# Four loads tied to the products of earlier chunks, two loads cut in half, and a relu ahead of a conversion

## The chip, the core and the metric

The kernel runs on one core of a Trainium2 chip. The metric is the device time of one execution in microseconds. The core has five engines with an instruction stream each: TensorE (PE in the profile; its weight loads are listed apart as PEld), VectorE (DVE), ScalarE (ACT), GpSimd (POOL) and SyncE (SP). SP does no arithmetic here, it issues every DMA of the kernel, one after the other in the order of its stream. The transfers themselves run on 16 DMA engines.

## The reference

A retention layer (a linear recurrence over 768 steps, 4 batches, 8 heads of dimension 64) is followed by a feed-forward layer with a relu, a convolution over three time steps and a sigmoid gate.

```python
def _attn_ref(q, k, v):
    gamma = 1.0 - 2.0 ** (-5.0 - np.arange(H))
    state = np.zeros((B, H, D, D))
    for t in range(S):
        state = gamma[None, :, None, None] * state + np.einsum('bhd,bhe->bhde', k[:, :, t], v[:, :, t])
        y[:, :, t] = np.einsum('bhd,bhde->bhe', q[:, :, t], state) / np.sqrt(D)
    return y

def _moe_ref(x, w_in, conv_w, w_out):
    h = np.maximum(x @ w_in, 0.0)            # [4, 768, 512] @ [512, 1024]
    conv_out = sum over k of conv_w[k] * (h shifted by k - 1 along time, zero at the ends)
    gate = 1.0 / (1.0 + np.exp(-conv_out))
    return h * gate @ w_out                  # [1024, 512]
```

The weights arrive as float64 and are converted on the chip.

## The kernel before, in words

The retention is computed in chunks of 64 time steps. A chunk number n stands for two batches and 64 steps, so there are 24 chunks. For a chunk, four blocks lie side by side in one tile `rw`: q and k with the head dimension on the partitions (slots 0 and 1), and k and v with time on the partitions (slots 2 and 3); a fifth slot takes the state carried over from the chunk before. One slot pair, 0 and 1 or 2 and 3, is 512 KB. There are three `rw` tiles, used in turn, so a chunk takes the tile of the chunk three before it.

The steps of chunk n, by their names in the code:

- `load/n` (L342) brings slots 0 and 1 for the first four chunks and for the chunks in `IN_TWO`, and all four slots (1 MB) for the others. `load_kv/n` (L352) brings slots 2 and 3 where `load` brought half.
- `scores/n` (PE, L410, tile `ps_s`) multiplies k by q. For the chunks from 4 on these products are emitted inside `mix/(n-1)`. There is one `ps_s` buffer: `scores/n` can start only when `masked/(n-1)` has read it.
- `masked/n` (DVE, L437) puts the masked scores back into slot 1; `scale_v/n` (ACT, L378) scales v in slot 3.
- `mix/n` and `across/n` (PE, L410, tiles `ps_y` and `ps_st`) make the output of the chunk and add to the state; `carry/n` (ACT, L444) copies the state; `decay/n` (DVE, L451), `x_head/n` (ACT, L461) and `x_rest/n` (DVE, L467) turn the output into two parts, a rounded one and the rest, for the next layer.

The weights are loaded in 16 pieces (`load_w/0` to `/7` the first matrix, `/8` to `/15` the second; `/16` is the convolution). Piece i goes through a row of conversions: `w_abs/i` (ACT, L495), `w_clamp/i`, `w_shift/i`, `w_sign/i`, `w_power/i` (DVE, L500 to L521), `w_head/i` (ACT, L546), `w_low/i`, `w_rest/i`, `w_add/i` (DVE, L529, L561, L576).

The first product `mm1/u/f` (PE, L590, tile `ps_m`) works on units u of two chunks and on pieces f of the weights; `relu/u/p` (ACT, L602) empties a `ps_m` buffer, of which there are two. Convolution, gate and second product follow and are not touched by the change.

At the very start PE has nothing to multiply, so six products on zeros are emitted (`fill`, L330), and three more ahead of `mix/0` (L324).

The order of all steps is written out by hand as the string `ORDER`: the steps are emitted in that order, and each engine executes its own instructions in the order in which they were emitted. An instruction waits only for the data and the buffers it needs. Besides this there is a table `HELD`: a step that stands in it as a key waits in addition until the last instruction of the step named beside it has finished. All keys of it are DMA loads. As SP works through its stream in order, whatever is queued on SP behind a held load waits too.

Of the kernel before, what the change touches and what calls it, by code (L numbers as in the profile page):

```python
# [61 lines left out]
HELD = {  # L62
    "load_kv/2": "mix/0", "load_kv/3": "make_gy/0", "load/7": "w_low/4", "load_w/4": "w_abs/3",
# [22 lines left out]
    w_shift/0 w_sign/0 w_abs/1 w_power/0 w_head/0 w_clamp/1 w_rest/0 scores/0 w_low/0 masked/0 scale_v/0 w_add/0
    w_shift/1 w_abs/2 mix/0 w_sign/1 w_clamp/2 w_shift/2 carry/0 load_kv/2 scores/1 w_power/1 load/3 w_head/1
    load_w/3 masked/1 load_w/16 scale_v/1 w_low/1 w_sign/2 mix/1 decay/0 across/1 make_gy/0 carry/1 w_head/2
    w_rest/1 load_kv/3 scores/2 load/4 decay/1 scale_v/2 masked/2 x_head/0 w_add/1 scores/3 x_head/1 w_power/2
    w_abs/3 x_rest/0 mix/2 x_rest/1 load_w/4 w_clamp/3 across/2 scale_v/3 w_shift/3 masked/3 mm1/0/0 load/5 w_low/2  # L90
    load_w/5 w_rest/2 mm1/0/1 w_sign/3 decay/2 w_head/3 w_add/2 carry/2 mix/3 w_abs/16 w_power/3 w_abs/4 w_rest/3
    across/3 x_head/2 masked/4 relu/0/0 w_low/3 mm1/0/2 load/6 scale_v/4 w_add/3 x_rest/2 mm1/0/3 carry/3 decay/3
    w_clamp/4 x_head/3 w_shift/4 mix/4 w_abs/5 x_rest/3 relu/0/1 w_clamp/5 across/4 make_gy/1 load_w/6 load_w/7
    mm1/1/0 w_shift/5 w_sign/4 w_sign/5 w_head/4 mm1/1/1 w_power/4 carry/4 w_power/5 w_head/5 masked/5 mm1/1/2
    scale_v/5 w_rest/4 w_clamp/16 w_low/4 relu/1/0 mm1/1/3 w_shift/16 load/7 scale_v/6 w_sign/16 w_add/4 w_power/16
    w_low/5 mix/5 relu/1/1 decay/4 w_abs/6 w_rest/5 across/5 w_clamp/6 w_low/16 w_add/5 mm1/1/4 carry/5 load/8
    decay/5 load_w/8 x_head/4 masked/6 w_abs/7 mm1/0/4 w_shift/6 w_add/16 w_sign/6 w_power/6 w_head/6 mix/6
    make_gy/2 conv_tap/0/2 across/6 w_clamp/7 scale_v/7 w_shift/7 masked/7 mm1/0/5 load/9 load_w/9 w_sign/7 carry/6
    conv_tap/0/3 w_low/6 mm1/1/5 relu/0/2 w_rest/6 w_head/7 seam/0/2/0 w_power/7 seam/0/1/0 w_add/6 mix/7 w_rest/7
    w_abs/8 across/7 w_low/7 x_head/5 relu/1/2 w_add/7 mm1/0/6 load/10 x_rest/4 w_clamp/8 x_rest/5 mm1/0/7 w_shift/8  # L100
    scale_v/9 w_sign/8 mm1/2/0 relu/0/3 masked/8 w_abs/9 scale_v/8 carry/7 mm1/2/1 w_power/8 w_head/8 load_w/10
    w_clamp/9 conv_tap/0/0 load_w/11 decay/7 mm1/1/6 w_shift/9 w_low/8 w_sign/9 mix/8 decay/6 w_head/9 scale_v/10
    across/8 masked/9 seam/0/0/0 seam/0/2/2 seam/1/2/0 mix/9 x_head/6 x_head/7 carry/8 w_power/9 relu/2/0
# [21 lines left out]
    conv_tap/1/6 gate/1/2 w_add/12 decay/14 diff/0/0/3 gated/1/2 seam/3/1/2 g_head/0/3 g_rest/0/3 conv_tap/1/2
    mm2/0/1/2/0 w_rest/15 w_add/15 conv_side/1/2/2 g_head/1/2 conv_tap/1/7 conv_side/1/6/0 masked/15 conv_tap/1/3
    scale_v/15 sum_w/0/7 conv_side/1/7/0 conv_side/1/6/2 relu/5/1 mm2/0/0/2/0 mm2/0/1/3/0 mm2/0/0/3/0
    conv_side/1/3/0 conv_side/1/7/2 conv_side/1/2/0 conv_side/1/3/2 gate/1/1 put/0/1/0 g_rest/1/2 gated/1/1
    g_head/1/1 load/16 mix/15 seam/6/3/0 seam/3/0/0 gate/1/3 across/15 carry/15 conv_tap/2/4 conv_tap/2/5 mm1/5/4
    mm1/5/5 seam/2/3/2 scale_v/16 diff/0/0/1 seam/3/2/0 mm2/1/0/0/0 g_rest/1/1 mm2/1/0/1/0 mm2/1/0/2/0 gated/1/3  # L130
    conv_side/2/4/2 sum_w/0/0 conv_tap/2/0 conv_side/2/0/2 g_head/1/3 g_rest/1/3 conv_tap/2/2 put/0/0/0 mm2/1/1/0/0
    mm2/1/1/1/0 diff/0/0/2 conv_side/2/5/2 sum_w/0/8 sum_w/0/9 conv_side/2/5/0 decay/15 conv_side/2/4/0 masked/16
    gate/2/2 conv_tap/2/1 head/0/0/0 decay/13 diff/0/1/3 conv_side/2/0/0 gated/2/2 g_head/2/2 diff/0/1/1
    conv_side/2/1/2 conv_side/2/1/0 conv_side/2/2/0 load/17 scale_v/17 g_rest/2/2 conv_tap/2/6 conv_tap/2/7
    conv_tap/2/3 mix/16 across/16 carry/16 relu/4/3 seam/3/3/2 head/0/1/0 gate/2/0 load/18 scale_v/18 mm2/1/1/2/0
    mm2/1/1/3/0 masked/17 mix/17 seam/5/3/2 seam/3/2/2 seam/5/2/2 seam/5/1/0 conv_side/2/7/0 conv_side/2/2/2
    across/17 conv_side/2/6/0 decay/16 conv_side/2/3/2 conv_side/2/3/0 gate/2/1 store/0/0/0 x_head/12 carry/17
    load/19 load_kv/19 masked/18 mm2/1/0/3/0 mix/18 across/18 seam/5/2/0 gated/2/1 g_head/2/1 seam/3/0/2 store/0/1/0
    gated/2/0 g_head/2/0 sum_w/0/1 put/1/1/0 store/1/1/0 g_rest/2/1 decay/17 relu/5/2 conv_tap/3/2 seam/6/1/0
    seam/4/3/0 seam/4/1/2 diff/0/1/2 g_rest/2/0 scale_v/19 put/1/0/0 store/1/0/0 conv_side/3/2/0 decay/18 diff/1/0/3  # L140
    x_head/13 conv_tap/3/4 conv_side/3/4/0 conv_tap/3/5 conv_side/3/5/0 carry/18 conv_tap/3/3 conv_side/3/3/0
    conv_side/2/7/2 conv_side/3/2/2 masked/19 load/20 conv_side/2/6/2 sum_w/0/2 conv_side/3/3/2 scale_v/20 gate/3/1
    gated/3/1 x_rest/13 mm1/5/6 load/21 mm1/5/0 mm1/5/1 mm1/5/7 head_rest/0/0/0 g_head/3/1 relu/5/0 mm2/2/0/0/0
    mm2/2/1/0/0 mm2/2/1/1/0 mix/19 masked/20 gate/2/3 conv_side/3/5/2 g_rest/3/1 across/19 mix/20 scale_v/21
    conv_tap/3/0 conv_tap/3/1 conv_side/3/4/2 decay/19 conv_side/3/0/2 gated/2/3 gate/3/2 conv_side/3/1/2
    conv_side/3/1/0 mm2/2/0/1/0 mm2/2/1/2/0 mm2/2/0/2/0 g_head/2/3 carry/19 sum_w/1/0 g_rest/2/3 mm2/2/0/3/0
    mm2/2/1/3/0 across/20 head/0/1/1 gated/3/2 conv_side/3/0/0 seam/5/1/2 relu/5/3 masked/21 conv_tap/4/0 g_head/3/2
    g_rest/3/2 gate/3/0 gated/3/0 x_rest/12 load/22 scale_v/22 conv_tap/4/1 mix/21 diff/0/1/4 conv_tap/4/2
    conv_side/4/2/2 g_head/3/0 g_rest/3/0 carry/20 across/21 conv_tap/3/6 seam/5/3/0 conv_tap/3/7 conv_side/4/1/0
# [5 lines left out]
    seam/5/0/0 gate/4/1 w_rest_t/0/1 sum_w/0/3 conv_tap/4/6 store/2/1/0 mm2/3/1/2/0 mm2/3/1/3/0 put/3/1/0 head/0/1/2
    conv_tap/4/5 conv_side/4/4/2 sum_w/0/4 conv_side/4/6/0 mix/22 masked/23 across/22 carry/22 store/3/1/0
    head/0/0/2 scale_v/23 w_head_t/1/1 conv_side/4/5/0 gated/4/1 decay/22 g_head/4/1 conv_side/4/4/0 mm2/3/0/3/0
    mm2/4/0/0/0 mix/23 seed/0/0 put/3/0/0 w_head_t/0/2 head/0/0/1 w_rest_t/1/1 sum_w/1/3 diff/1/1/3 sum_w/1/4
    w_head_t/1/2 across/23 decay/23 conv_side/4/5/2 conv_tap/4/7 prod/0/0/2 w_rest_t/1/2 g_rest/4/1 w_rest_t/0/2
# [727 lines left out]
```

## Time and profile before

| | |
|---|---|
| time of three executions | 329.06, 329.79 (median), 330.97 us |
| the profiled execution: own time, span | 330.33 us, 328.6 us |
| granted TensorE clock over the span | 0.999 of full speed |
| busy DVE, ACT, POOL | 288.3, 214.6, 25.8 us (88%, 65%, 8%) |
| DMA | 40.77 MB |
| idle time of PE before `ps_s` products, and whom it ended with | 1.7 us DVE, 1.0 us "issue" |
| idle time of DVE before `masked` | 5.1 us, ended by PE |

The span is what the profile covers; the execution's own time is 1.73 us longer. The busy time of an engine is the time in which one of its instructions runs. "Idle before" is the time for which an engine stood still ahead of an instruction, and the arrow names what ended it; "issue" means that the profile shows nothing that the engine waited for. Windows are given in microseconds from the start of the span.

### The profile page before, as it was taken

The numbers are of one execution on the slowest core, as the hardware profiler recorded it, in microseconds if no ns is written. First come the engines' busy times: TensorE is split into PE (matmuls) and PEld (weight loads), VectorE is DVE, ScalarE is ACT, GpSimd is POOL, SyncE is SP. The second block draws the span as 40 slices with busy tenths as digits, with TensorE's granted clock in tenths as the row PEclk, the third lists the DMA queues.
The fourth block names the chain that finished last, engine by engine and source line by source line (L and its number), as shares of the span: only waits on it lengthen the run. The fifth ranks groups of instructions, "written<-read, shape, count | busy, mean of one in ns | idle before, by whom it ended". The sixth has DMA issues, their size and how long they took to land.

```text
span 328.6 us, 10761 instructions
## 1 busy us (share of the span) xinstructions
PE 320.6 (98%) x4642; PEld 286.2 (87%) x4642; DVE 288.3 (88%) x566; ACT 214.6 (65%) x448; POOL 25.8 (8%) x100
## 2 busy tenths in 40 slices
...
GB/s 250 349 362 324 212 312 284 254 78 256 192 106 279 133 19 144 128 253 151 90 194 34 34 0 35 34 2 0 32 34 0 65 0 65 3 64 0 66 64 64
DMA packets 10559, 40.77 MB, mean 124 GB/s; under 512 B 1296, under 2 KB 1808, under 8 KB 8080
## 3 DMA queue, kind: packets, MB, share of 16 engines
...
q8 instruction: 36, 0.59, 0.7%
...
## 4 chain that ended last, share of the span: by engine, by line
PE 89%; DVE 8%; ACT 1%; issue 1%; ACTq 0%; DVEq 0%
PE ps_o L808 39%; PE ps_m L590 16%; PE ps_m L711 8%; PE ps_y L711 8%; PE ps_s L410 5%; PE ps_st L410 4%; PE ps_y L410 3%; PE ps_o L330 3%; PE ps_s L711 2%; DVE cv L773 1%; DVE m L513 1%; DVE rw L437 1%; DVE g L529 1%; DVE cv L784 1%; PE ps_o L324 0%
## 5 line engine op out<-in xcount | busy, mean ns | idle before, releaser
L590 PE MATMUL ps_m<-xu,wi_hi 128*128 128x256 f32 x384 | 67.9, 281 | 0.2 <-ACT h_u L602 0.2
L808 PE MATMUL ps_o<-h,g 128*128 128x512 f32 (+1 forms) x200 | 62.3, 381 | 0.0
L590 PEld LDWEIGHTS ps_m<-xu,wi_hi 128*128 128x128 f32 x384 | 57.9, 188 | 1.4 <-ACT h_u L602 0.4
L590 PE MATMUL ps_m<-xu,wi_lo 128*128 128x256 f32 x192 | 53.2, 277 | 0.0
L779 ACT ACTIVATE cv<-cv 128x512 f32<-128x512 f32 x48 | 29.9, 630 | 33.7 <-DVE cv L773 33.6
L410 PE MATMUL ps_y<-rw 64*64 64x64 f32 x1472 | 48.5, 220 | 0.0
L410 PEld LDWEIGHTS ps_y<-rw 64*64 64x64 f32 x1472 | 45.1, 135 | 0.5 <-ACT rw L644 0.4
L808 PEld LDWEIGHTS ps_o<-h,g 128*128 128x128 f32 x200 | 37.2, 188 | 6.7 <-ACT o_sb L815 0.2
L773 DVE SCALAR_TENSOR_TENSOR cv<-h,cw_sb,cv 128x256 f32<-128x256 f32 x84 | 38.7, 478 | 1.0 <-ACT cv L768 0.4
L794 DVE TENSOR_TENSOR g<-cv,g 128x512 fp32r<-128x512 f32 x48 | 32.6, 687 | 7.0 <-ACT g L789 6.3
L789 ACT CAST g<-cv 128x512 fp32r<-128x512 f32 x48 | 29.3, 617 | 11.9 <-DVE cv L784 10.5
L590 PEld LDWEIGHTS ps_m<-xu,wi_lo 128*128 128x128 f32 x192 | 36.0, 188 | 0.0
L410 PEld LDWEIGHTS ps_s<-rw 64*64 64x64 f32 x768 | 24.6, 135 | 7.5 <-issue 3.2
L410 PE MATMUL ps_s<-rw 64*64 64x64 f32 x768 | 27.8, 221 | 2.7 <-DVE rw L437 1.7
L410 PE MATMUL ps_st<-rw 64*64 64x64 f32 x704 | 25.3, 219 | 0.9 <-ACT rw L378 0.5
L410 PEld LDWEIGHTS ps_st<-rw 64*64 64x64 f32 x704 | 22.9, 135 | 2.1 <-issue 0.9
L378 ACT ACTIVATE rw<-rw,consts_sb 128x128 f32<-128x128 f32 x64 | 20.4, 390 | 4.9 <-DMA rw<-in_qkv 4.8
L768 ACT ACTIVATE cv<-h,cw_sb 128x256 f32<-128x256 f32 x42 | 20.4, 503 | 2.0 <-DVE g L794 2.0
L437 DVE TENSOR_TENSOR rw<-ps_s,consts_sb 128x512 f32<-128x512 f32 x24 | 16.4, 684 | 5.1 <-PE ps_s L410 5.1
L815 ACT COPY o_sb<-ps_o 128x512 f32<-128x512 f32 (+1 forms) x25 | 13.9, 559 | 10.2 <-PE ps_o L808 10.2
L808 PE MATMUL ps_o<-h_g,g 128*128 128x512 f32 (+1 forms) x50 | 19.3, 388 | 0.0
L808 PE MATMUL ps_o<-h_s,g 128*128 128x512 f32 (+1 forms) x50 | 19.2, 385 | 0.0
(256 smaller groups left out, 756.1 us busy)
## 6 DMA issues: line engine op xcount, KB each, us to landing
...
```

The costliest lines, as they stand in the source:

```text
L378: nc.scalar.activation(v[:, :, g], v[:, :, g], AF.Copy, scale=by[:, g : g + 1])
L410: nc.tensor.matmul(out, lhsT, rhs, start=start, stop=stop, skip_group_check=True)
L437: nc.vector.tensor_tensor(out=rw[n][:, 1], in0=s_ps[n], in1=mask_sb.unsqueeze(1).broadcast_to([P, 2, NPAIR, C]), op=ALU.mult)
L590: nc.tensor.matmul(h_ps[u, p][:, odd], w[:, k, fs], x[:, k].rearrange("p b t -> p (b t)"), start=(i == 0), stop=(i == len(products) - 1),)
L711: nc.tensor.matmul(ps[:, i], w[k][:, fs], x[:, k].rearrange("p b t -> p (b t)"), start=(i == m == 0 and q in (1, 5)), stop=(m == len(produ ...
L768: nc.scalar.activation(cvs[u, p][:, i], hs[u, p][:, i, :, 1 : P + 1], AF.Copy, scale=cw_sb[:, f, 1:2])
L773: nc.vector.scalar_tensor_tensor(out=cv, in0=h[:, :, k : k + P], scalar=cw_sb[:, f, k : k + 1], in1=cv, op0=ALU.mult, op1=ALU.add)
L779: nc.scalar.activation(cvs[u, p], cvs[u, p], AF.Sigmoid)
L789: nc.scalar.copy(gs[u, p][:, 0], cvs[u, p])
L794: nc.vector.tensor_tensor(out=lo, in0=cvs[u, p], in1=hi.bitcast(F32), op=ALU.subtract)
L808: nc.tensor.matmul(ps, g, w[f][:, cs], start=(f == 0 and i == 0), stop=(f == NF - 1 and i == 2))
L815: nc.scalar.copy(o[:, :n], o_ps[u, t, h][:, :n])
```

## The change

Four entries are added to `HELD`, chunks 4 and 5 are added to `IN_TWO`, and the order is written anew. `load/2` and `load/3` bring the same bytes as before, but now wait for `mix/0` and `mix/1`. The loads of chunks 4 and 5, 1 MB each before, now bring q and k alone; their other halves become `load_kv/4` and `load_kv/5`, which stand behind `load_w/4` and behind `mix/3` in the order and wait for `mix/2` and `mix/3`. `relu/3/3` moves ahead of `w_abs/15` on ACT. The sequences of PE, DVE and POOL keep their order.

```diff
-IN_TWO = (19,)
+IN_TWO = (4, 5, 19)
...
 HELD = {
+    "load/2": "mix/0", "load/3": "mix/1", "load_kv/4": "mix/2", "load_kv/5": "mix/3",
...
-    load_w/0 load_w/1 load/0 load_consts load_kv/0 load_w/2 load/1 load_kv/1 load_gy load/2 w_abs/0 w_clamp/0
+    load_w/0 load_w/1 load/0 load_consts load_kv/0 load_w/2 load/1 load_kv/1 load_gy w_abs/0 w_clamp/0 w_shift/0
...
-    conv_side/1/5/2 conv_side/1/4/2 load_w/15 w_abs/15 w_clamp/15 w_shift/12 w_shift/15 w_low/14 w_sign/15
+    conv_side/1/5/2 conv_side/1/4/2 mm1/3/6 mm1/3/7 relu/3/3 load_w/15 w_abs/15 w_clamp/15 w_shift/12 w_shift/15
```

SP's stream before, from the second load of constants on. In order: `load_gy`, `load/2`, `load_kv/2`, `load/3`, `load_w/3`, `load_w/16`, `load_kv/3`, `load/4`, `load_w/4`, `load/5`, `load_w/5`, `load/6`.

```order
L361 DMA consts_sb<-in_consts 128x256
L349 DMA rw<-in_qkv 128x1024
L353 DMA rw<-in_qkv 128x1024
L349 DMA rw<-in_qkv 128x1024
L477 DMA g_262<-in_w_in 128x1024
L477 DMA cw_t<-in_conv_w 128x48
L353 DMA rw<-in_qkv 128x1024
L349 DMA rw<-in_qkv 128x2048
L477 DMA g_414<-in_w_in 128x1024
L349 DMA rw<-in_qkv 128x2048
L477 DMA g_455<-in_w_in 128x1024
L349 DMA rw<-in_qkv 128x2048
```

The same place of SP's stream now, from `load_kv/3` on (the file has one line more, so its line numbers are higher by one): `load_kv/3`, `load/4`, `load_w/4`, `load_kv/4`, `load/5`, `load_w/5`, `load_kv/5`, `load/6`.

```order
L354 DMA rw<-in_qkv 128x1024
L350 DMA rw<-in_qkv 128x1024
L478 DMA g_414<-in_w_in 128x1024
L354 DMA rw<-in_qkv 128x1024
L350 DMA rw<-in_qkv 128x1024
L478 DMA g_456<-in_w_in 128x1024
L354 DMA rw<-in_qkv 128x1024
L350 DMA rw<-in_qkv 128x2048
```

Two transfers of 128x2048 became two pairs of 128x1024. Ahead of this place SP's stream has the same transfers in the same sequence as before; what changes there is only what `load/2` and `load/3` wait for, and with SP working in order, `load_kv/2` stands behind the held `load/2`, and `load_w/3` and `load_w/16` behind the held `load/3`.

ACT's stream before, around `relu/3/3` (`h_u`), `w_abs/12` (`m_1940`) and `w_abs/15` (`m_1952`); `h_m` is the second matrix's piece written by `w_head/12`, `h_v` is `relu/4/0`.

```order
L495 ACTIVATE m_1940<-g_1926 128x512
L768 ACTIVATE cv_1945<-h_1055,cw_sb 128x256 x2
L495 ACTIVATE m_1952<-g_1950 128x512
L602 ACTIVATE h_u<-ps_m_1961 128x4x128
L546 CAST h_2012<-m_1952 128x512
L444 COPY rw<-ps_st 128x512
L546 CAST h_m<-m_1940 128x512
L602 ACTIVATE h_v<-ps_m_1987 128x4x128
```

And now.

```order
L496 ACTIVATE m_1942<-g_1928 128x512
L769 ACTIVATE cv_1947<-h_1057,cw_sb 128x256 x2
L603 ACTIVATE h_u<-ps_m_1952 128x4x128
L496 ACTIVATE m_1980<-g_1978 128x512
L547 CAST h_2014<-m_1980 128x512
L445 COPY rw<-ps_st 128x512
L547 CAST h_m<-m_1942 128x512
L603 ACTIVATE h_v<-ps_m_1989 128x4x128
```

The third and the fourth instruction have changed places; the rest stands as it stood.

## Rows read from the trace of the kernel before

**Rows 1.** The page: PE busy; instruction queue (packets, MB, share); the chain by engine.
```profile
PE 320.6 (98%) x4642; PEld 286.2 (87%) x4642; DVE 288.3 (88%) x566; ACT 214.6 (65%) x448; POOL 25.8 (8%) x100
...
q8 instruction: 36, 0.59, 0.7%
...
PE 89%; DVE 8%; ACT 1%; issue 1%; ACTq 0%; DVEq 0%
```

**Rows 2.** Timeline of PE: start, us, what, count, [idle before <-releaser].
```profile
16.24 0.23 PE L410 MATMUL ps_st<-rw 64*64 64x64 f32 x2
16.25 0.98 PE L410 MATMUL ps_y<-rw 64*64 64x64 f32 x28
...
17.19 0.98 PE L410 MATMUL ps_s<-rw 64*64 64x64 f32 x27
...
19.85 0.33 PE L410 MATMUL ps_s<-rw 64*64 64x64 f32 x4 [1.68 <-DVE rw L437]
...
27.73 0.27 PE L410 MATMUL ps_s<-rw 64*64 64x64 f32 x2 [0.96 <-issue]
...
61.31 0.27 PE L410 MATMUL ps_st<-rw 64*64 64x64 f32 x1 [0.45 <-issue]
...
103.01 0.50 PE L590 MATMUL ps_m<-xu,wi_hi 128*128 128x256 f32 x2 [0.15 <-ACT h_u L602]
```

**Rows 3.** Windows, between the two unexplained stops: us, busy and count per engine, clock, DMA.
```profile
26.90:61.10 34.20, 33.13 (x894) 32.02 (x893) 32.80 (x66) 23.00 (x52) 2.06 (x6) 1.00 0.78 279
```

**Rows 4.** Timeline of SP: load/2, load_kv/2, load/3, load_w/3, load/4, load_w/4.
```profile
6.31 0.65 SPq L349 DMA_DIRECT2D rw<-in_qkv  x1
13.19 0.33 SPq L353 DMA_DIRECT2D rw<-in_qkv  x1
13.70 0.33 SPq L349 DMA_DIRECT2D rw<-in_qkv  x1
14.08 1.10 SPq L477 DMA_DIRECT2D g<-in_w_in  x1
...
18.46 0.37 SPq L349 DMA_DIRECT2D rw<-in_qkv  x1
21.15 0.33 SPq L477 DMA_DIRECT2D g<-in_w_in  x1
```

**Rows 5.** Source lines, landings of load/2, load_kv/2, load/3, load_w/3, load_w/4, load_w/0.
```profile
DMA to landing us min/median/max: 9.6/9.6/9.6
...
DMA to landing us min/median/max: 4.3/4.3/4.3
...
DMA to landing us min/median/max: 5.3/5.3/5.3
...
DMA to landing us min/median/max: 6.2/6.2/6.2
...
DMA to landing us min/median/max: 6.3/6.3/6.3
...
DMA to landing us min/median/max: 3.4/3.4/3.4
```

**Rows 6.** Timeline of DVE: masked/2, w_clamp/3, masked/4.
```profile
19.11 0.68 DVE L437 TENSOR_TENSOR rw<-ps_s,consts_sb 128x512 f32<-128x512 f32 x1
...
21.85 0.41 DVE L500 TENSOR_SCALAR m<-m 128x512 f32<-128x512 f32 x1
...
28.22 0.69 DVE L437 TENSOR_TENSOR rw<-ps_s,consts_sb 128x512 f32<-128x512 f32 x1 [0.76 <-PE ps_s L410]
```

**Rows 7.** Timeline of ACT: w_abs/3, and w_abs/15 with relu/3/3.
```profile
20.42 0.70 ACT L495 ACTIVATE m<-g 128x512 f32<-128x512 f32 x1 [0.58 <-DVE wi_lo L576]
...
101.80 0.68 ACT L495 ACTIVATE m<-g 128x512 f32<-128x512 f32 x1
102.38 0.58 ACT L602 ACTIVATE h_u<-ps_m 128x512 f32<-128x512 f32 x1
```

**Rows 8.** Timeline of DVE: w_clamp/15, the second of two L500 steps here.
```profile
102.97 0.42 DVE L500 TENSOR_SCALAR m<-m 128x512 f32<-128x512 f32 x1
```

**Rows 9.** The chain that ended last: what holds the next relu, h_v.
```profile
107.49 0.60 ACT h_v L602
```

More of the change, by code (lines that the diff above doesn't have):

```diff
@@ L84 @@
 ORDER = """
-    load_w/0 load_w/1 load/0 load_consts load_kv/0 load_w/2 load/1 load_kv/1 load_gy load/2 w_abs/0 w_clamp/0
[L86 to L103, printed above, removed]
+    load_w/0 load_w/1 load/0 load_consts load_kv/0 load_w/2 load/1 load_kv/1 load_gy w_abs/0 w_clamp/0 w_shift/0
@@ new lines @@
+    w_sign/0 w_abs/1 w_power/0 w_head/0 w_clamp/1 w_rest/0 scores/0 w_low/0 masked/0 scale_v/0 w_add/0 w_shift/1
+    w_abs/2 mix/0 w_sign/1 w_clamp/2 w_shift/2 carry/0 load/2 load_kv/2 scores/1 w_power/1 w_head/1 masked/1
+    scale_v/1 w_low/1 w_sign/2 mix/1 load/3 load_w/3 load_w/16 decay/0 across/1 make_gy/0 carry/1 w_head/2 w_rest/1
+    load_kv/3 scores/2 load/4 decay/1 scale_v/2 masked/2 x_head/0 w_add/1 scores/3 x_head/1 w_power/2 w_abs/3
+    x_rest/0 mix/2 x_rest/1 load_w/4 load_kv/4 w_clamp/3 across/2 scale_v/3 w_shift/3 masked/3 mm1/0/0 load/5
@@ new lines @@
+    w_low/2 load_w/5 w_rest/2 mm1/0/1 w_sign/3 decay/2 w_head/3 w_add/2 carry/2 mix/3 load_kv/5 w_abs/16 w_power/3
+    w_abs/4 w_rest/3 across/3 x_head/2 masked/4 relu/0/0 w_low/3 mm1/0/2 load/6 scale_v/4 w_add/3 x_rest/2 mm1/0/3
+    carry/3 decay/3 w_clamp/4 x_head/3 w_shift/4 mix/4 w_abs/5 x_rest/3 relu/0/1 w_clamp/5 across/4 make_gy/1
+    load_w/6 load_w/7 mm1/1/0 w_shift/5 w_sign/4 w_sign/5 w_head/4 mm1/1/1 w_power/4 carry/4 w_power/5 w_head/5
+    masked/5 mm1/1/2 scale_v/5 w_rest/4 w_clamp/16 w_low/4 relu/1/0 mm1/1/3 w_shift/16 load/7 scale_v/6 w_sign/16
@@ new lines @@
+    w_add/4 w_power/16 w_low/5 mix/5 relu/1/1 decay/4 w_abs/6 w_rest/5 across/5 w_clamp/6 w_low/16 w_add/5 mm1/1/4
+    carry/5 load/8 decay/5 load_w/8 x_head/4 masked/6 w_abs/7 mm1/0/4 w_shift/6 w_add/16 w_sign/6 w_power/6 w_head/6
+    mix/6 make_gy/2 conv_tap/0/2 across/6 w_clamp/7 scale_v/7 w_shift/7 masked/7 mm1/0/5 load/9 load_w/9 w_sign/7
+    carry/6 conv_tap/0/3 w_low/6 mm1/1/5 relu/0/2 w_rest/6 w_head/7 seam/0/2/0 w_power/7 seam/0/1/0 w_add/6 mix/7
+    w_rest/7 w_abs/8 across/7 w_low/7 x_head/5 relu/1/2 w_add/7 mm1/0/6 load/10 x_rest/4 w_clamp/8 x_rest/5 mm1/0/7
@@ L104 @@
+    w_shift/8 scale_v/9 w_sign/8 mm1/2/0 relu/0/3 masked/8 w_abs/9 scale_v/8 carry/7 mm1/2/1 w_power/8 w_head/8
+    load_w/10 w_clamp/9 conv_tap/0/0 load_w/11 decay/7 mm1/1/6 w_shift/9 w_low/8 w_sign/9 mix/8 decay/6 w_head/9
+    scale_v/10 across/8 masked/9 seam/0/0/0 seam/0/2/2 seam/1/2/0 mix/9 x_head/6 x_head/7 carry/8 w_power/9 relu/2/0
     conv_tap/0/1 conv_side/0/0/0 w_rest/8 w_add/8 load/11 seam/2/0/0 conv_tap/0/4 seam/5/0/2 seam/0/1/2 seam/0/0/2
@@ L125 @@
[L125 to L149, printed above, removed]
@@ L155 @@
[L155 to L159, printed above, removed]
@@ new lines @@
+    w_low/14 w_sign/15 w_power/15 w_rest/14 mm1/4/0 mm1/4/1 w_head/15 w_sign/12 carry/13 w_head/12 relu/4/0 w_add/14
+    w_power/12 w_low/12 w_rest/12 conv_side/1/4/0 seam/1/3/2 mm1/4/2 mm1/4/3 relu/4/1 load/15 x_rest/10 mix/14
+    across/14 mm1/4/6 mm1/4/7 g_head/1/0 carry/14 g_rest/1/0 mm1/5/2 mm1/5/3 w_low/15 conv_side/1/5/0 conv_tap/1/6
+    gate/1/2 w_add/12 decay/14 diff/0/0/3 gated/1/2 seam/3/1/2 g_head/0/3 g_rest/0/3 conv_tap/1/2 mm2/0/1/2/0
+    w_rest/15 w_add/15 conv_side/1/2/2 g_head/1/2 conv_tap/1/7 conv_side/1/6/0 masked/15 conv_tap/1/3 scale_v/15
```

51 lines of the change are left out of this document (38 added, 13 removed).

## The prediction

> **What bounds the kernel now.** I read the page first. PE is busy for 320.6 of 328.6 us, and the chain that ended last is 89% PE and 8% DVE [rows 1]. So little can be won: everything that PE does not use is 8 us, a good part of it before the first data. Next I read the timeline of PE for its stops. After the first products there are four that bear on this change [rows 2]: 1.68 us before `scores/3` at 19.85, ended by DVE; 0.96 us at 27.73 in the middle of `mix/3` and 0.45 us at 61.31, both ended by nothing that the profile shows ("issue"); and 0.15 us at 103.01, ended by `relu/3/3`. No stop of PE after 19.85 is put down to a data load.
>
> The two unexplained stops look like one thing. Between them PE ran 894 products and 893 weight loads [rows 3], 1,787 instructions. The queue that brings instructions moved 0.59 MB in 36 packets [rows 1], 16.4 KB each; PE's 2 x 4,642 instructions [rows 1] over 36 packets are 258 per packet, and 1,787 is close to seven packets (1,806). So both stops are, by my reading, PE at the end of a packet with the next one not there yet. If a packet is asked for when the one before it is begun, the one missing at 26.77 was asked for at about 21.5: half a packet is 129 products, of which some 75 stand between 22.9 and 26.77 (an estimate from the timeline). What lay in the DMA queue then? `load_w/4`, issued at 21.15, landed 6.3 us later, at 27.45 [rows 4, 5]; PE went on at 27.73, just behind it. The DMA queue thus seems to be where the packet was stuck, and the change alters what is in that queue.
>
> **The change part by part.** The sum is made on the profiled execution, 330.33 us, which is 0.54 above the median of the three runs (329.79).
>
> *load/2, from 6.31 to behind mix/0.* `load_kv/2` was held to `mix/0` already and issued at 13.19 [rows 4], so `load/2` now goes at 13.19 and `load_kv/2` some 0.4 later. `load_w/0`, with an empty queue, landed in 3.4 us [rows 5]; a load with more ahead of it took 4.3 to 5.3. So `load/2` lands at 16.6, at worst at 18.5 (it landed at 15.9 before). `scores/2` ran from 17.02 to 18.17 (its last 27 products start at 17.19 and take 0.98) [rows 2], and `masked/2`, in DVE's queue behind other work, began only at 19.11 [rows 6]. `scores/2` may therefore be 0.9 late for nothing, and at the worst landing it ends at 19.65, 0.54 late. I take 0; ends 0 and +0.5. What stood ahead of `load/2` on the queue loses nothing by its absence, and gains nothing: it was behind them.
>
> *load/3, from 13.70 to behind mix/1.* `mix/1` ends with the products at 16.24 and 16.25 [rows 2], so `load/3` goes at about 16.45, 2.75 later. Only `load_kv/2` is then ahead of it. With 3.4 us it lands at 19.85, with the 4.3 of `load_kv/2` at 20.75, with its own old 5.3 at 21.75. `scores/3` started at 19.85, the moment `masked/2` freed the scores' buffer. So the slack is used up. I take the near row, 3.4, and 0.2 for the signal and the transfer ahead: +0.2. Ends 0 and +1.9. PE goes without a stop from 19.85 to 26.77, so this is on the path.
>
> *load_w/3 behind it.* It stands behind `load/3` on SP, and landed 1.3 later than that (20.3 against 19.0, rows 4, 5). It now lands at about 21.2; `w_abs/3` moves from 20.42 [rows 7] to 21.25, ends at 21.95, and `w_clamp/3` from 21.85 [rows 6] to 22.0. DVE is 0.15 late; what covers it is the 0.76 that DVE idles before `masked/4` at 28.22 [rows 6]. Cost 0. With `load/3` at 21.75 DVE would be 2.0 late and the cover gone by 1.2, which lies beside PE's own 1.9.
>
> *Chunks 4 and 5 in halves.* `load/4` still goes at 18.46 [rows 4] but with half the bytes. At the 1.3 us between the landings of `load/3` and `load_w/3` for one 512 KB transfer, `load/4` is in 1.3 earlier. `load_w/4` is held to `w_abs/3` and goes 0.8 later, at 21.95. The half taken out comes back at about 22.3 as `load_kv/4`, lands some 26.6 by the same 1.3 each, and is first read by `scale_v/4` for `mix/4`, which also needs `masked/4` of 28.22 [rows 6]. The same holds for chunk 5. Cost of these two themselves: 0; two more issues of some 0.4 us on SP lie in SP's waiting time.
>
> *The stop at 26.77.* If the packet waits behind what was issued before it, then at 21.7 there is `load/4`'s half, landing near 23.7, and not `load_w/4`, which goes at 21.95; even behind `load_w/4`, which now lands near 25.4, the packet is there before 26.77. Then 0.96 is won. Ends -0.96 and 0. I take -0.96. PE then reaches `scores/4` earlier, DVE's 0.76 of waiting at 28.22 shrinks, and from there PE and DVE both run ahead.
>
> *relu/3/3 before w_abs/15.* The relu goes to 101.80 and ends 0.58 earlier [rows 7], so the 0.15 at 103.01 goes. But the chain does not pass there: in this stretch it runs through DVE's queue to `w_head/12` on ACT and to the relu behind it, `h_v`, at 107.49 [rows 9], and PE waits for that one anyway. `w_abs/15` starts some 0.5 later and ends at about 102.97, just when DVE wants it for `w_clamp/15` [rows 8], a link of that chain. So nothing is won, and 0 to 0.1 is lost: +0.05.
>
> Sum: 0.2 - 0.96 + 0.05 = -0.7. From 330.33 that is 329.6, from the median 329.1.
>
> **The rivals.** *The packet stays late (or another one is).* For it speaks that the DMA engines are as full as before in this stretch, so that a packet that takes turns with the data gets no quicker through; against it, that PE resumed right behind the last landing. The packet before it, asked for one packet earlier in PE's stream (near 16.7, an estimate), now has `load/3` and `load_w/3` issued around its request, and could be late at 21.5. Then only +0.25 is left: 330.0. The Trainium skill, on the page "DMA: Bandwidth & Descriptors", section "Queues, rings and completion order", says that a DMA engine takes turns between its queues packet by packet; by that rule instructions do not stand behind the whole data queue, the stop would stay, and the time would be this rival's. The trace leaves it open: the stop at 61.31 came after a quieter stretch and was shorter.
>
> *load/3 is late.* A mechanism for the other side: SP issues `load/3` only at 16.45 and it lands as it did, 5.3 us later. `scores/3` and all of PE behind it is 1.9 late, and with the packet asked for later as well, nothing is won at 26.77: +1.95, 331.7. It turns the forecast's sign from a landing of about 20.75 on. For it: transfers behind others took 4.3 and more. Against: here only one transfer is ahead.
>
> *Both stops go.* If the loads shift so that the packet at 60.86 is in time too, and `load/3` is punctual: -0.96 - 0.45 + 0.05 = -1.4, 328.4. Against: nothing in the change touches the loads ahead of that stop.
>
> That the change does not do what it says can be left out for the holds: the streams show them. For the relu it is the likeliest case.
>
> **How the numbers follow.** Forecast 0.47, packet stays late 0.27, `load/3` late 0.14, both stops 0.12. What a measurement can tell from no change is about 0.5%, 1.65 us here. Forecast and packet case are inside it; the late load is outside for most of its part, the last case for a part, and I add a little on both sides for stops that no row shows: faster 0.14, same 0.73, slower 0.13. The range takes in the packet case and most of the two others: 328.0 to 331.2.
>
> **What would show it.** Right: `load/2` issued near 13.2 and landed before 17.5; `scores/3` within 0.5 of 19.85 in its new place; no stop in `mix/3` near 26.8; DVE's wait before `masked/4` near zero; the stop at 103 gone and PE's next wait for `h_v` at least as long. Wrong: a stop of PE before `scores/3` ended by a DMA and longer than 0.5; a stop marked "issue" of 0.5 or more between 20 and 30; or a gain larger than the two stops, which would mean that the data ahead of `load/2` landed sooner without it.

## The result: slower by 0.8%, and the profile after

| | before | after |
|---|---|---|
| median of 20 executions each | 330.18 us | 334.13 us |
| lowest, highest | 328.9, 335.9 us | 329.58, 338.32 us |
| ratio, 95% interval | | 1.0082 [1.0058, 1.0107] |
| profiled execution: time, span, granted clock | 330.33 us, 328.6 us, 0.999 | 329.58 us, 327.8 us, 1.000 |

The kernel became slower; the predicted 329.1 us and its range up to 331.2 were wrong. The ratio leaves disturbed executions out (nine of the 20 of after), so it need not agree with the two medians.

The profiled execution is the fastest of the 20, and it misleads: it is 0.75 us shorter than the profiled one of before, as if the forecast had come true. The others spread by their mean granted clock: the eight at 0.997 or above took 329.6 to 334.3 us (median 332.7), the twelve below it 333.1 to 338.3 (median 337.2). So there are two losses to explain: some 2.5 us at the full clock, and some 4.5 more in the executions with the lower one, of which the clock itself need not be all. Of 124 executions of before timed beside the experiments, 15 had a clock below 0.997.

The page of after (PE, instruction queue, chain by engine), against [rows 1]:

```profile
PE 319.7 (98%) x4642; PEld 286.1 (87%) x4642; DVE 288.2 (88%) x566; ACT 214.8 (66%) x448; POOL 26.0 (8%) x100
...
q8 instruction: 36, 0.59, 0.7%
...
PE 85%; DVE 6%; DMA 4%; ACT 1%; SPq 1%; issue 1%; ACTq 0%
```

The work is the same. What is new is the 4% of DMA in the chain: loads now end waits of PE. The timeline of PE in after, the stops that answer to [rows 2] (start, us, what, count, [idle before <-releaser]):

```profile
17.13 1.15 PE L411 MATMUL ps_s<-rw 64*64 64x64 f32 x32 [0.49 <-DMA rw<-in_qkv]
...
20.19 1.09 PE L411 MATMUL ps_s<-rw 64*64 64x64 f32 x30 [1.91 <-DMA rw<-in_qkv]
...
106.95 0.50 PE L591 MATMUL ps_m<-xu,wi_hi 128*128 128x256 f32 x2 [0.46 <-ACT h_v L603]
```

`scores/2` waits for `load/2`, and `scores/3` for `load/3`, where DVE ended its wait before. No stop marked "issue" of 0.2 us or more is left: the 0.96 and the 0.45 of [rows 2] are gone, and the 0.15 at `h_u` has become 0.46 at `h_v`. SP in after, against [rows 4]: `load/2`, `load_kv/2`, `load/3`, `load_w/3`, and further down `load/4`, `load_w/4`, `load_kv/4`.

```profile
12.26 0.33 SPq L350 DMA_DIRECT2D rw<-in_qkv  x1
12.64 0.43 SPq L354 DMA_DIRECT2D rw<-in_qkv  x1
15.83 0.33 SPq L350 DMA_DIRECT2D rw<-in_qkv  x1
16.20 0.43 SPq L478 DMA_DIRECT2D g<-in_w_in  x1
...
18.83 0.38 SPq L350 DMA_DIRECT2D rw<-in_qkv  x1
22.14 0.33 SPq L478 DMA_DIRECT2D g<-in_w_in  x1
22.56 0.38 SPq L354 DMA_DIRECT2D rw<-in_qkv  x1
```

Landings of the first four in after, against [rows 5]:

```profile
DMA to landing us min/median/max: 4.7/4.7/4.7
...
DMA to landing us min/median/max: 5.6/5.6/5.6
...
DMA to landing us min/median/max: 4.2/4.2/4.2
...
DMA to landing us min/median/max: 5.1/5.1/5.1
```

`load/2` lands at 12.26 + 4.7 = 16.96, within what was told (16.6 to 18.5), and `load/3` at 15.83 + 4.2 = 20.03. `masked/2` on DVE had freed the scores' buffer at 19.02, so of the 1.91 us before `scores/3` the last 1.17 are the late load's; before it was 0.06. On DVE, against [rows 6], `w_clamp/3` waits for `w_abs/3` of the later `load_w/3`, and `masked/4` no longer waits for anything:

```profile
22.15 0.43 DVE L501 TENSOR_SCALAR m<-m 128x512 f32<-128x512 f32 x1 [0.75 <-ACT m L496]
...
27.69 0.68 DVE L438 TENSOR_TENSOR rw<-ps_s,consts_sb 128x512 f32<-128x512 f32 x1
```

ACT in after, against [rows 7]: `relu/3/3` now stands ahead of `w_abs/15`, and `h_v`, against [rows 9], at 106.30.

```profile
100.60 0.59 ACT L603 ACTIVATE h_u<-ps_m 128x512 f32<-128x512 f32 x1
101.08 0.67 ACT L496 ACTIVATE m<-g 128x512 f32<-128x512 f32 x1
...
106.30 0.59 ACT L603 ACTIVATE h_v<-ps_m 128x512 f32<-128x512 f32 x1
```

Why is this execution not slower? It began better, in work that the change leaves alone. The products on zeros at the start, in before:

```profile
1.05 8.39 PE L330 MATMUL ps_o<-o_sb 128*128 128x512 f32 x12 [1.05 <-DVE o_sb L316]
```

and in after:

```profile
1.05 7.46 PE L331 MATMUL ps_o<-o_sb 128*128 128x512 f32 x12 [1.05 <-DVE o_sb L317]
```

That is 0.93 us, and over all eighteen profiles this group takes 6.95 to 8.39 us, with no pattern by kernel. In spite of it `scores/3` starts 0.34 later than before (20.19 against 19.85), so 0.93 + 0.34 = 1.27 us were lost up to there. Then +0.34 - 0.96 - 0.45 + 0.31 (the relu) = -0.76, the 0.8 between the spans. One profile from the end of a wide spread had hidden a loss behind a lucky start. Its lines were less kind than its time: most signs that the prediction named for being right are there (no stop near 26.8, no wait before `masked/4`, the stop at `h_u` gone), but so is its first sign of being wrong, a stop before `scores/3` that a DMA ends and that is longer than 0.5.

### The profile page after: what moved, and what is told of

Its sections match the earlier page's. It is cut to its first block, busy times and chain, and to the rows that moved or that the text cites. A ratio compares the mean times of both kernels' runs of the same rounds, so it can differ in the third digit from the quotient of the medians.

```text
span 327.8 us, 10766 instructions
## 1 busy us (share of the span) xinstructions
PE 319.7 (98%) x4642; PEld 286.1 (87%) x4642; DVE 288.2 (88%) x566; ACT 214.8 (66%) x448; POOL 26.0 (8%) x100
## 4 chain that ended last, share of the span: by engine, by line
PE 85%; DVE 6%; DMA 4%; ACT 1%; SPq 1%; issue 1%; ACTq 0%
PE ps_o L809 40%; PE ps_m L591 16%; PE ps_m L712 8%; PE ps_y L712 8%; PE ps_s L411 5%; DMA rw<-in_qkv 4%; PE ps_st L411 4%; PE ps_y L411 3%; PE ps_s L712 2%; DVE cv L774 1%; DVE m L514 1%; DVE cv L785 1%; DVE m L501 0%; DVE g L530 0%; DVE g L795 0%
## 5 line engine op out<-in xcount | busy, mean ns | idle before, releaser
L411 PE MATMUL ps_s<-rw 64*64 64x64 f32 x768 | 27.5, 221 | 2.6 <-DMA rw<-in_qkv 2.6
```

The costliest lines, as they stand in the source:

```text
L411: nc.tensor.matmul(out, lhsT, rhs, start=start, stop=stop, skip_group_check=True)
```

## The experiments

Each ran beside runs of the kernel before on the same chip. The theories: the loads come late because the hold of `load/2` lets the DMA queue run empty (the gap, G where a letter stands for it; H is the wait that the holds make, C the clock, S and P the halves); the granted clock falls behind the longer wait; instruction packets are late at other places than before; the relu. The rival to all of them was that the result belonged to that group of executions and not to the kernel.

**The changed kernel again.** No edit.

> The changed kernel once more, to see the spread of its executions and, if the profile is of another execution than the first, where a longer one loses its time. Theory H (the holds of load/2 and load/3 make PE wait for data at 12 to 20 us, and the length of that wait differs from execution to execution): median about 333, executions from 329.5 to 338, and a profile above 331 shows stops of PE ended by DMA before scores/1 to scores/3 of more than the 2.6 us of the first profile. Theory C (on top of H, the granted TensorE clock falls for a stretch in some executions): the mean granted clock below 0.997 in the longer ones, with the fall behind a stop of PE. Rival S (the halves of chunks 4 and 5 cost it): stops of PE or half-filled stretches after 25 us.

Median 335.21 us (6 executions, 332.41 to 337.03), ratio 1.016 [1.0117, 1.0203], all six with a clock of 0.989 to 0.994. So the loss belongs to the kernel. Its profile has both losses. Timeline of PE, three stops:

```profile
21.97 1.87 PE L411 MATMUL ps_s<-rw 64*64 64x64 f32 x30 [3.82 <-DMA rw<-in_qkv]
...
45.30 0.21 PE L411 MATMUL ps_y<-rw 64*64 64x64 f32 x1 [0.30 <-issue]
...
65.83 0.27 PE L411 MATMUL ps_st<-rw 64*64 64x64 f32 x1 [0.95 <-issue]
```

Windows of it (us, busy and count of PE, PEld, DVE, ACT, POOL, clock, DMA share, GB/s):

```profile
13.00:14.00 1.00, 1.00 (x40) 0.88 (x31) 0.97 (x3) 0.87 (x2) 0.00 (x0) 1.00 0.08 23
...
22.00:23.00 1.00, 1.00 (x20) 1.00 (x22) 0.89 (x2) 0.09 (x1) 0.00 (x0) 0.50 1.03 410
...
21.95:45.00 23.05, 22.93 (x583) 22.10 (x584) 19.81 (x40) 14.20 (x34) 0.00 (x0) 0.88 0.84 281
```

The same products in the profile of after, and the stretch at 13 in after and in before:

```profile
20.17:40.60 20.43, 20.39 (x583) 19.74 (x584) 19.43 (x39) 14.20 (x34) 0.00 (x0) 1.00 0.85 303
...
13.00:14.00 1.00, 0.56 (x20) 0.42 (x15) 0.53 (x2) 0.76 (x3) 0.00 (x0) 1.00 0.60 189
```

```profile
13.00:14.00 1.00, 0.92 (x36) 0.85 (x30) 0.97 (x3) 0.86 (x2) 0.00 (x0) 1.00 0.75 283
```

Between 13 and 14 the queue has run empty: 23 GB/s, where before, with `load/2` long in it, moved 283. `load/2` lands at 16.88, `load_kv/2` 2.87 later, `load/3` another 2.05 later, at 21.80. PE stands for 3.82 us, and in this wait the granted clock drops to 0.50, the 1.2 GHz level, and stays there up to 27.5. That costs 23.05 - 20.43 = 2.62 us over 583 products that have no stop of 0.15 us or more in either profile. With the later start of `scores/3` (21.97 against 20.19) and two late packets (0.30 and 0.95) it makes 1.78 + 2.62 + 1.25 = 5.65 us, and the spans differ by 5.6. Of the 1.78 some 0.9 may be the slower start (8.38 us for the products on zeros, 7.46 in after).

The same kernel did better in the first profile, with the queue low as well (189 GB/s): there `load_kv/2` landed 1.3 us behind `load/2`. What differs is how long SP takes to issue `load_kv/2`, 0.43 us there and 1.32 here:

```profile
13.55 1.32 SPq L354 DMA_DIRECT2D rw<-in_qkv  x1
```

The eight profiles with `load/2` held to `mix/0` fall into two groups. In four the issue of `load_kv/2` takes 0.43 us, its landing is 1.3 us behind that of `load/2`, and the queue moves 156 GB/s or more between 13 and 14; in the other four the issue takes 1.14 to 1.49 us, the landing is 2.3 to 2.9 us behind, and the queue moves 149 or less. Whether the low queue makes the issue long is not shown.

**The halves of chunks 4 and 5 alone.**

```diff
 (before)
-IN_TWO = (19,)
+IN_TWO = (4, 5, 19)
+    "load_kv/4": "mix/2", "load_kv/5": "mix/3",
```

> The kernel before with only chunks 4 and 5 loaded in halves, the second halves held to mix/2 and mix/3. Theory H and C: no loss, since load/2 and load/3 go early as before; if the packet of instructions stood behind load_w/4 in the queue, load_w/4 now still goes at 21.15, with 512 KB less ahead of it, and the stop in mix/3 shrinks from 0.96 to 0 or little: ratio 0.997 to 1.000. Rival S: ratio 1.006 to 1.01, the whole loss of the change.

331.10 us (12), 1.0021 [0.9981, 1.006]: not told from no change, and between the two expectations. Timeline of PE, its stops marked "issue":

```profile
21.22 0.21 PE L411 MATMUL ps_st<-rw 64*64 64x64 f32 x1 [0.30 <-issue]
...
32.09 0.27 PE L411 MATMUL ps_s<-rw 64*64 64x64 f32 x2 [0.90 <-issue]
...
37.19 0.39 PE L591 MATMUL ps_m<-xu,wi_hi 128*128 128x256 f32 x2 [0.42 <-issue]
...
43.96 0.21 PE L411 MATMUL ps_y<-rw 64*64 64x64 f32 x1 [2.22 <-issue]
```

Windows between them, and inside the last:

```profile
21.21:31.20 9.99, 9.97 (x254) 9.48 (x254) 9.68 (x18) 7.08 (x17) 0.00 (x0) 1.00 0.95 346
32.08:36.78 4.70, 4.67 (x128) 4.52 (x128) 4.70 (x10) 2.81 (x7) 0.00 (x0) 1.00 0.75 261
37.18:41.75 4.57, 4.55 (x127) 4.29 (x127) 3.06 (x9) 2.55 (x7) 0.00 (x0) 1.00 0.69 246
...
42.00:43.00 1.00, 0.00 (x0) 0.00 (x0) 0.42 (x1) 0.00 (x0) 0.00 (x0) 1.00 0.00 0
```

Products and weight loads together, 508, 256 and 254 instructions stand between the stops: two, one and one packet of 256. In all eighteen profiles the stops marked "issue" of 0.25 us or more sit on such steps, after 222, 348, 475, 602, 730, 857, 985 or 1369 products, within one. The Trainium skill, on the page "Runtime: NRT & Kernel Launch", section "Instruction fetch mechanics", says that instructions are refilled in blocks of 256, at a cost that is mostly hidden; the first agrees with these rows, the second holds for most of the 36 packets of an execution, but one step here cost 2.22 us.

The trace also has the packets themselves, on queue q8. The DMA view of 0.1 us, from 41.7 in this run and from 25.4 in before (packets, MB, share of 16 engines):

```profile
q8 instruction: 1, 0.02, 60.0%
```

```profile
q8 instruction: 1, 0.02, 59.6%
```

So a packet starts at 41.72 and takes 0.96 us (60% of 16 engines for 0.1 us), and PE goes on at 43.96, 1.28 us after its end; the windows above count a transfer where it starts, which is why the one from 42 to 43 shows nothing. In before the packet runs from 25.41 to 26.36, and PE goes on at 27.73, 1.37 later. All 48 stops marked "issue" of 0.15 us or more in the eighteen profiles end 1.20 to 1.58 us after the end of a packet, and it is the packet whose turn it is by the count. That these stops are late packets is thereby shown. When a packet was asked for is not in the trace, nor what holds it until it starts.

The stop after 475 products, the 0.96 of before, is gone, as it is in all ten profiles with chunk 4 halved; of the eight others five have it. In before its packet starts 3.9 us after PE has begun the packet ahead of it (at 21.47), in after 1.1 us (at 21.76). But others came.

**One hold at a time.**

```diff
 (before, hold of load/2)
+    "load/2": "mix/0",
 (before, hold of load/3; load_w/3 and load_w/16 behind it)
+    "load/3": "mix/1",
```

> The kernel before with only load/2 held to mix/0 and moved behind carry/0. If the late load/2 alone makes the loss: ratio 1.005 to 1.01 with PE waiting for it before scores/2. If only load/3 does: 0.998 to 1.002. A gain of up to 0.9 us would come if load/0, load/1 and their second halves land earlier without load/2 in the queue (in the first profile of the changed kernel they landed 0.7 to 0.9 us earlier).

> The kernel before with only load/3 held to mix/1, and load_w/3 and load_w/16 behind it. Theory H: a wait of PE before scores/3 of 0.2 to 2 us ended by DMA, ratio 1.002 to 1.006. If both holds are needed for the loss (the waits add up to a stop that brings the clock down): 1.000 to 1.002. If load/3 alone brings it about: 1.006 to 1.01 and executions up to 338.

`load/2` alone: 331.92 us (12), 1.0043 [1.0016, 1.0069], 8 of 12 clocks below 0.997. `load/3` alone: 330.82 (12), 1.0037 [1.0014, 1.006], 9 of 12. Stops of PE in the first:

```profile
21.78 1.09 PE L411 MATMUL ps_s<-rw 64*64 64x64 f32 x30 [3.18 <-DMA rw<-in_qkv]
...
24.38 0.21 PE L411 MATMUL ps_st<-rw 64*64 64x64 f32 x1 [0.79 <-issue]
```

and in the second, with a window of it:

```profile
16.72 0.62 PE L411 MATMUL ps_y<-rw 64*64 64x64 f32 x14 [0.90 <-issue]
...
19.37 1.86 PE L411 MATMUL ps_s<-rw 64*64 64x64 f32 x30 [1.09 <-DMA rw<-in_qkv]
```

```profile
20.00:22.00 2.00, 2.00 (x64) 2.00 (x62) 1.51 (x3) 0.68 (x1) 0.00 (x0) 0.50 1.00 348
```

The first was expected to make PE wait before `scores/2`; the wait came before `scores/3`. Holding `load/2` makes `load/3` late though `load/3` itself is not held: it is issued at 14.99 and lands at 21.69, and `scores/3` starts 1.9 us behind the end of `masked/2`. Held itself, with `load/2` early, it is issued at 15.61 and lands at 19.21, and `scores/3` starts 0.35 behind `masked/2`. The clock does not follow the length of the wait alone: no fall behind 3.18 us here, a fall around 0.90 and 1.09 there.

**Both holds without the rest, and the changed kernel without load/3's hold.**

```diff
 (before)
+    "load/3": "mix/1",
+    "load/2": "mix/0",
 (after)
-    "load/2": "mix/0", "load/3": "mix/1", "load_kv/4": "mix/2", "load_kv/5": "mix/3",
+    "load_kv/4": "mix/2", "load_kv/5": "mix/3",
+    "load/2": "mix/0",
```

> The kernel before with both holds (load/2 to mix/0, load/3 to mix/1, load_w/3 and load_w/16 behind it) and nothing else. Theory H (the loss is the late arrival of load/3 at PE, made by the two holds together): ratio 1.006 to 1.015, the whole loss of the change, with a stop of PE before scores/3 ended by DMA of 2 to 4 us. Rival S (the halves of chunks 4 and 5 matter as much): 1.000 to 1.004.

> The changed kernel with load/3, load_w/3 and load_w/16 at their old places and load/3 not held; the hold of load/2, the halves and the relu stay. Theory H with load/3 as the main cause: most of the loss gone, ratio 1.000 to 1.005. If the empty DMA queue that the held load/2 leaves near 13 us is the main cause: 1.004 to 1.01, since load/3 still lands behind load/2 and load_kv/2 near 19.5 to 21.7.

Both holds: 332.52 us (12), 1.0068 [1.0041, 1.0095], 9 of 12 clocks low; `load/3` lands at 22.01, and PE waits 3.15. That is most of the 0.8% of the first measurement, and under half of the 1.6% of the repeated one. The other: 335.75 (6), 1.0174 [1.0145, 1.0204], 5 of 6 low, where 1.010 was the most that was expected; `load/3`, issued at 14.72, lands at 22.42. Taking load/3's hold out does not help while load/2's stays, and this one is worse than the sum of its parts, which stays unexplained.

**Three zero products ahead of `scores/3`**, on the changed kernel, on before, and (last) on both holds: they fill the wait and change no result (the buffer table gets a slot for them).

```diff
-    "mix/0": 3,
+    "mix/0": 3, "scores/3": 3,
```

> The changed kernel with three products on zeros ahead of scores/3 on PE (1.56 us by the row of the three before mix/0; PE waits there at least 1.4 us in every profile so far). Theory C (in many executions the granted clock falls to 0.50 during that wait and costs 2 to 3 us afterwards): no stretch at 0.50 any more, ratio 1.002 to 1.006, the executions above 335 gone. Without theory C (only the wait counts): no change, 1.008 to 1.016.

> The kernel before with the same three products on zeros ahead of scores/3. They fit into the wait of 1.68 us that ends with masked/2. Theory C: the kernel before has its few long executions (to 335.9) from the same fall of the clock; the median goes down by 0 to 1 us and the longest executions fall away: 0.996 to 1.000. Without theory C: 1.000, with the same spread.

> The kernel with both holds and no halves (r5, 1.0068), with three products on zeros ahead of scores/3. Theory C (the fall of the granted clock is part of that loss): the mean clock is 0.998 or more in nearly all executions, ratio 1.002 to 1.005. Without it (only the wait for load/3 counts): 1.006 to 1.008.

Changed kernel: 332.52 us (8), 1.008 [1.0045, 1.0115], 1 of 8 clocks low; the clock did what was expected, the ratio (1.002 to 1.006 if the clock were the larger part) did not. Before: 330.77 (12), 1.0031 [1.0003, 1.0059], 0 of 12; a miss, it was not to get slower. In its profile the products end at 20.24, when `load/3` (19.29) and `masked/2` (19.49) are long done, so there they hold `scores/3` back. Both holds: 331.87 (12), 1.0037 [1.0005, 1.0069], 1 of 12 where there had been 9 (on another chip). The window of the changed kernel that answers to the 0.50 above:

```profile
22.00:24.00 2.00, 2.00 (x85) 1.93 (x75) 1.00 (x4) 0.93 (x2) 0.00 (x0) 1.00 0.89 348
```

So the clock falls because PE stands idle there, and 332.52 is what the eight executions of after at full clock took (332.7). The other 2.5 us stay.

**The gap by itself:** the changed kernel without load/2's hold, with `load_w/3` in load/2's old place, and with `load/2` held to `scores/0`.

```diff
-    "load/2": "mix/0", "load/3": "mix/1", "load_kv/4": "mix/2", "load_kv/5": "mix/3",
+    "load_kv/4": "mix/2", "load_kv/5": "mix/3",
+    "load/3": "mix/1",
...
-    ... load_gy w_abs/0 ... load/3 load_w/3 load_w/16
+    ... load_gy load_w/3 w_abs/0 ... load/3 load_w/16
...
-    "load/2": "mix/0", "load/3": "mix/1", "load_kv/4": "mix/2", "load_kv/5": "mix/3",
+    "load/2": "scores/0", "load/3": "mix/1", "load_kv/4": "mix/2", "load_kv/5": "mix/3",
```

> The changed kernel with load/2 back at its old place and not held; the hold of load/3, the halves and the relu stay. Theory G (the hold of load/2 is what makes load/3 late: behind it the DMA queue runs empty near 13 us and the next three transfers land 1.3 to 2.9 us apart): load/3 lands at 19 to 19.8, the stop before scores/3 is 2 us or less, ratio 1.001 to 1.006. Theory H (the hold of load/3 matters as much): load/3 at 20.5 or later, ratio 1.008 to 1.016.

> The changed kernel with load_w/3 issued in the place that load/2 had before (it needs no wait there); load/2 and load/3 stay held. Theory G with the empty queue as the cause: the queue does not run empty, load/2, load_kv/2 and load/3 land about 1.3 us apart, load/3 near 19.5 to 20.2, ratio 1.000 to 1.006. If what counts is only that load/2 and load_kv/2 are issued together behind mix/0, whatever is in the queue: load/3 at 20.5 to 22.4, ratio 1.008 to 1.016.

> The changed kernel with load/2 held to scores/0 (which ends near 10.5) in place of mix/0 (near 13), so that it is issued before the queue runs empty near 14. Theory G: like r9, load/3 lands at 19 to 20, ratio 1.000 to 1.006. If any held load/2 is bad: 1.008 to 1.016.

| | us (12 each) | ratio | load/3 lands | wait before scores/3 | scores/3 behind the end of masked/2 |
|---|---|---|---|---|---|
| not held | 333.16 | 1.0075 [1.004, 1.011] | 19.55 | 1.18 | 0.44 |
| gap filled | 332.73 | 1.0083 [1.005, 1.0116] | 20.09 | 1.36 | 0.64 |
| held to scores/0 | 333.17 | 1.0072 [1.004, 1.0105] | 19.14 | 1.65 | 0.71 |

The profile names DVE for the second and the third of these waits, but what `scores/3` needs of DVE had long been done. PE and DVE of the second:

```profile
20.19 1.09 PE L411 MATMUL ps_s<-rw 64*64 64x64 f32 x30 [1.36 <-DVE wi_lo L577]
...
18.86 0.69 DVE L438 TENSOR_TENSOR rw<-ps_s,consts_sb 128x512 f32<-128x512 f32 x1 [0.19 <-PE ps_s L411]
```

`masked/2` ends at 19.55, and PE starts 0.1 us behind the landing of `load/3`, as in the profiles where the DMA is named. So `load/3` still ends the wait, but later than DVE by only 0.4 to 0.7 us; in the repeated run it was 2.5, in the run with `load/2` alone held 1.9.

The landing did what the gap theory said: 1.6 to 3.3 us earlier than the 21.69 to 22.42 of the runs above. It varies by itself, though: with the gap open it was 20.03 in the first profile and 20.49 with the zero products. The time did not follow, and all three ratios lie above the 1.006 that the gap theory allowed. The gap alone falls as the cause of the time; in these profiles late packets took its place. Stops of PE in the first of the three:

```profile
16.91 0.62 PE L412 MATMUL ps_y<-rw 64*64 64x64 f32 x14 [1.04 <-issue]
...
22.84 0.21 PE L412 MATMUL ps_st<-rw 64*64 64x64 f32 x1 [1.37 <-issue]
33.16 0.27 PE L412 MATMUL ps_s<-rw 64*64 64x64 f32 x2 [0.34 <-issue]
...
45.58 0.21 PE L412 MATMUL ps_y<-rw 64*64 64x64 f32 x1 [1.94 <-issue]
```

These are 4.69 us of late packets; the other two have 4.52 and 3.24. The eight profiles with both halves held have 2.6 us of such stops on average (0 to 4.7), the seven with no halves 1.35 (0 to 2.7). That is a lean of some 1.2 us, from one profile each.

**The relu alone,** in before:

```diff
-    load_w/15 w_abs/15 ... mm1/3/6 mm1/3/7 relu/3/3
+    mm1/3/6 mm1/3/7 relu/3/3 load_w/15 w_abs/15 ...
```

> The kernel before with only relu/3/3 moved ahead of w_abs/15. As predicted: the stop of 0.15 before the product behind relu/3/3 is gone and comes back at the relu behind it (h_v): 0.999 to 1.001. If this swap has a part in the loss: 1.002 or more.

330.49 us (12), 1.0024 [0.9991, 1.0058]. This is above the 1.001 expected of a swap that costs nothing, but its interval takes in no change. The wait for `h_u` is gone, and the next one is the one that the changed kernel has:

```profile
106.79 0.51 PE L590 MATMUL ps_m<-xu,wi_hi 128*128 128x256 f32 x2 [0.46 <-ACT h_v L602]
```

The 0.46 is in all eight profiles with the relu moved. The ten without have 0.16 to 0.22 at `h_u` and 0.06 to 0.12 at `h_v`, so moving it costs 0.13 to 0.25 us.

**The halves apart:** both halves but not held, only chunk 4, only chunk 5.

```diff
 (both, not held)
-IN_TWO = (19,)
+IN_TWO = (4, 5, 19)
-    ... load/4 ... load/5 ...
+    ... load/4 load_kv/4 ... load/5 load_kv/5 ...
 (chunk 4)
+IN_TWO = (4, 19)
+    "load_kv/4": "mix/2",
 (chunk 5)
+IN_TWO = (5, 19)
+    "load_kv/5": "mix/3",
```

> The kernel before with chunks 4 and 5 loaded in halves, the second half issued directly behind the first and not held: the bytes move when they moved before. Theory P (the halves cost because their held bytes come later and fill the queue while instruction packets are asked for): no stop marked issue near 602, 730 or 857 products, ratio 0.999 to 1.002. If two transfers more, of smaller pieces, are the cause: stops there as in r2, ratio 1.002 to 1.005.

> The kernel before with only chunk 4 in halves, the second held to mix/2. Theory P: the stop after 475 products is gone or small, since less is in the queue then; at 602 (begun near 27, when load_kv/4 is on its way) a stop is possible, at 730 and 857 none: ratio 0.997 to 1.002. This is the one part that could come out ahead of the kernel before.

> The kernel before with only chunk 5 in halves, the second held to mix/3. Theory P: the stop after 475 products stays (0.4 to 1 us), and stops come at 730 and 857: ratio 1.002 to 1.006. If the stops at 730 and 857 have nothing to do with load_kv/5: 1.000.

Not held: 330.42 us, 1.0008 [0.9977, 1.004]; no packet is late at 602, 730 or 857 products, two are earlier. Chunk 4: 330.05, 1.0009 [0.9979, 1.0039]; stops at 602 (0.69) and 985 (0.43), none at 475. Chunk 5: median 332.92, 1.001 [0.9971, 1.0048], where 1.002 to 1.006 with stops at 730 and 857 had been expected (there is one at 857, 0.29, and the 475 stays); six of its twelve executions lie at 333.9 to 335.4, with clocks of 0.990 to 0.998, and why is open. None of the three differs from before by more than can be told. A late packet at 602, 730 or 857 is in nine of the ten profiles with a held half and in none of the eight others, so these stops come with the held halves; that they cost time is not proved by the times. No version tried was faster than the kernel before.

## Why the prediction was wrong, step by step

- **load/2's hold, 0 (ends 0 and +0.5): the step that failed.** Its own landing came as told (16.96, and `scores/2` waited 0.49). The prediction looked at what stood ahead of `load/2` on the queue, which "loses nothing by its absence", and put at nothing what the hold does to the loads behind it. In truth `load/2` was what kept the queue full up to `mix/0`. Without it the next two landings come 2.9 and 2.1 us apart in the repeated run, against 1.6 and 1.5 before [rows 4, 5], and `load/3` is at 21.69 even where it is not held. Alone the hold costs 0.43%. That the queue ran low is shown; that this is the whole cause is not, since the first profile has landings 1.3 and 1.8 apart with a low queue too, and since loads early again left the time as it was.
- **load/3's hold, +0.2 (ends 0 and +1.9): too small.** The 3.4 was the row of the first transfer, in an empty queue; measured were 3.6 to 5.4 wherever it was held. PE waited 1.91 in the fastest execution and 3.82 in another, of which 1.68 was there before, for DVE [rows 2]. In that other one the rival "load/3 is late" came true almost to the digit: issue at 16.45 and 5.3 us to landing were told, 16.40 and 5.4 measured. Its place and price were right, its chance of 0.14 was too small, and it ended where the clock's loss begins.
- **The granted clock: no term at all.** The prediction priced a wait by its length. Here a wait of PE costs a second time, 2.62 us in one profile, for products that then run at 0.50. Executions with the low clock were longer than the others of the same kernel by 0.5 to 4.5 us (medians, where there are three or more of both), so longer waits or other stops may go with it. The wait of 1.68 in before mostly stays without this; the longer ones and the ones beside a late packet often do not.
- **load_w/3, 0:** its wait moved to DVE as told (0.75 before `w_clamp/3`), beside PE's own wait. Right.
- **The stop at 26.77, -0.96:** right that it was a late packet, that the stops are whole packets apart, and that halving `load/4` takes it away: it is in none of ten profiles with the half, and in five of eight without. Wrong was what the packet stood behind: it had come in at 26.36, before `load_w/4` (27.45), and it started just after `load/4` had landed (25.29); that PE went on right behind the landing of `load_w/4` was chance. The size was that of one execution; in the other four it is 0.42 to 0.65. Late packets elsewhere took it back, as the first rival said in its brackets ("or another one is"). That rival rested on turns taken between queues; that its packet started 3.9 us after PE had begun the one ahead of it in before and 1.1 in after speaks for waiting behind data. In after it ran while `load/4` was still on its way (landed at 24.00), so neither picture is settled.
- **relu, +0.05:** right in kind, too small. PE did not wait for `h_v` "anyway": 0.06 us in before, 0.46 with the relu moved. It costs 0.13 to 0.25, from 0 to 0.1 expected.
- **The two halves "themselves 0":** not told from 0 (1.0021, 1.0008, 1.0009, 1.001).

The parts' ratios add to 1.0043 + 1.0037 for the holds against 1.0068 measured together, and with 1.0021 and 1.0024 to a loss of some 1.1%, between the two measurements of the whole, 0.8 and 1.6%. The 2.5 us at full clock can be put together as an estimate: 1.1 for `load/3` in the first profile, 1.2 for late packets and 0.2 for the relu. These are single profiles that spread as widely, so the split stays open.
